# The last 64 rows of two weight matrices: from full rows on 64 partitions, loaded by GpSimd, to half rows on 128 partitions, loaded by SyncE

## The chip, the core and the metric

One core of a Trainium2 chip. The metric is the time of one execution in microseconds (us) of the device, taken as the median of several runs. Lower is better. Input and output tensors lie in HBM; the kernel brings them into the core's on-chip memory (SBUF, 128 partitions) with DMAs, which run on 16 DMA engines. A DMA is issued by an engine's queue: here SP (SyncE), ACT (ScalarE) and POOL (GpSimd). PE is TensorE, DVE is VectorE.

## The reference, cut to what matters

```python
# x: (8, 1, 448); 16 query heads on 8 KV heads of 256; cache of 4096, the last W = 1024 are used
q = (x @ wq).reshape(B, 1, Hq, Dh).transpose(0, 2, 1, 3)     # wq: 448 x 4096
k, v = the last W rows of the caches, each KV head for two query heads
p = softmax(q @ k^T * Dh**-0.5)
a = (p @ v) as (B, 1, 4096) @ wo                             # wo: 4096 x 448
h = gelu(layernorm(x) @ w1 + b1)                             # w1: 448 x 1792
b = h @ w2 + b2                                              # w2: 1792 x 448
g = sigmoid((x * gate_w).sum(-1))
out = g * a + (1 - g) * b
```

Everything is bfloat16. The row count of wq and w1, 448, is 3 x 128 + 64: the last 64 rows are what the change is about.

## The kernel before, in words

**Loads.** `plan` is a list of loads in a fixed order, each into one of `RING = 9` slots of 128 x 8192 elements (2 MB). `pump()` issues loads until nine are ahead of what has been consumed; `done()`, called where a slot has been read for the last time, frees one and pumps again. The order: the keys of group 0 (in two halves), w1, wq in two slots (two thirds of the main rows, then the last third), w2, then keys and values of 16 groups of four KV heads (values three groups behind the keys, `LAG`), and at the end wo in two slots and six pieces (L171 to L187). All these are issued by SP in the order of the plan. Each DMA from SP or ACT uses one of eight completion counters in turn, so an issue waits until the DMA eight places earlier has landed; it also waits for the last reader of the slot's previous content.

**Rows of wq and w1.** The first 384 rows (`DM`) stand three to a partition: partition p holds rows 3p, 3p+1, 3p+2 (L161, L162). The last 64 (`DT`) go through `ends` (L125): two DMAs of 32 rows each, onto partitions 64 to 95 and 96 to 127 (`ER = 64`), as full rows behind the main rows in the slot. They are issued by POOL. Ahead of each of them POOL issues a DMA of a few bytes into an unused tile, `side` (`step_over`, L117). Within 32 partitions the rows are permuted: partition 4i + j holds row 8j + i.

**Compute at the start.** `ends_of` (L248) puts the last 64 columns of x, in that permutation, into columns 64 to 127 of a zeroed row tile `xz`, and of the normed y into `yz`. `transposed` (L241) brings x (and y) to the partitions with four PE transposes: three for the main rows, one for the tail. `query` (L356) multiplies: 128 matmuls, of which the last 32 contract over partitions 64 to 127. `mlp_hidden` (L468) does the same for w1: 42 matmuls for the main rows and 14 for the tail (L482), then the bias and gelu on DVE and ACT.

**The loop.** For each group, `transpose_keys` turns 32 key tiles (64 PE transposes, copied out by ACT and DVE), `values(u - 3)` multiplies an earlier group's probabilities by its values, `scores` and `top` do the scores and their maxima. PE's program is written out by hand in this order. After the last group: `values`, `finish`, `spread_rows`, and `project` (L578), 128 matmuls against wo, each waiting for its piece. One DVE instruction (L599) applies the gate, and four DMAs store the result.

Of the kernel before, what the change touches and what calls it, by code (L numbers as in the profile page):

```python
# [11 lines left out]
BF16 = mybir.dt.bfloat16  # L12
# [5 lines left out]
def kernel(  # L18
# [15 lines left out]
    nc = tc.nc  # L34
    P = nc.NUM_PARTITIONS

    NB, Sq, D = A_x.shape
    _, Hkv, Sk, Dh = A_k_cache.shape
    HD = A_wq.shape[1]
# [4 lines left out]
    F = B_w1.shape[1]  # L44
    assert (NB, Sq, D, Hkv, Dh, Hq, W, F) == (8, 1, 448, 8, 256, 16, 1024, 1792)
    NJ = Dh // P
    NC = W // P
    NR = 3
    DM = NR * P
    DT = D - DM  # L50
    NF = F // P
    QUAD = 4
    RQ = QUAD * rep
    NQ = NB * Hkv // QUAD
# [8 lines left out]
    WO_PARTS = [[(0, NJ8)]] * (NHQ - 1) + [[(0, 4), (4, 6), (6, 8)]]  # L63
    RING = 9
    LAG = 3
    ER = P - DT
    BIG = 1e30
    qscale = float(Dh) ** -0.5

    xf = A_x.rearrange("b s d -> (b s) d")  # L70
# [3 lines left out]
    consts = ctx.enter_context(tc.tile_pool(name="consts", bufs=1))  # L74
# [36 lines left out]

        return load

    side = consts.tile([NB, 8, 32], BF16)
    turns = [0]

    def step_over():  # L117
        i = turns[0]
        turns[0] += 1
        nc.gpsimd.dma_start(  # L120
            side[:, 2 * i : 2 * i + 2, 0:16],
            xf[:, 0:32].rearrange("b (a n) -> b a n", a=2),
        )

    def ends(t, o, src):  # L125
        n = src.shape[1]
        for h in range(DT // 32):
            rows = src[DM + 32 * h : DM + 32 * h + 32, :]
            step_over()
            nc.gpsimd.dma_start(  # L130
                t[ER + 32 * h : ER + 32 * h + 32, o : o + n],
                rows.rearrange("(j i) n -> i j n", i=NB),
            )

    def rows_loader(pieces, tail=None):
        def load(t):
            o = 0
            for ap in pieces:
                n = 1
                for s in ap.shape[1:]:  # L140
                    n *= s
                dst = t[:, o : o + n]
                if len(ap.shape) == 3:
                    dst = dst.rearrange("p (a n) -> p a n", a=ap.shape[1])
                nc.sync.dma_start(dst, ap)  # L145
                o += n
            if tail is not None:
                ends(t, o, tail)

        return load  # L150

# [2 lines left out]
    def add(key, loader):  # L154
        index[key] = len(plan)
        plan.append(loader)
# [2 lines left out]
        add((name, u), kv_loader(src, u, parts))  # L159

    wq_m = A_wq[0:DM, :].rearrange("(p r) n -> p (r n)", r=NR)  # L161
    w1_m = B_w1[0:DM, :].rearrange("(p r) f -> p (r f)", r=NR)  # L162
    w2_v = B_w2.rearrange("(p c) n -> p (c n)", c=NF)
    wo_v = A_wo.rearrange("(q p j) n -> p q (j n)", p=P, j=NJ8)

    add_kv("k", A_k_cache, 0, parts=2)
    add(("w1",), rows_loader([w1_m], B_w1))
    add(("wq", 0), rows_loader([wq_m[:, 0 : 2 * HD]]))
    add(("wq", 1), rows_loader([wq_m[:, 2 * HD : 3 * HD]], A_wq))
    add(("w2",), rows_loader([w2_v]))  # L170
    for u in range(1, NQ):  # L171
        add_kv("k", A_k_cache, u)
# [17 lines left out]
        return slots[index[key]]  # L190

    x_sb = consts.tile([NB, D], BF16)
    ident = consts.tile([P, P], BF16)
    make_identity(nc, ident[:])
    pump()
    nc.scalar.dma_start(x_sb[:], xf)
    gw_b = consts.tile([NB, D], BF16)
    b2_r = consts.tile([1, D], BF16)
    b1_sb = consts.tile([P, NF], BF16)
    nc.scalar.dma_start(  # L200
        gw_b[:], gate_w.rearrange("(o d) -> o d", o=1).to_broadcast([NB, D])
    )
    nc.scalar.dma_start(b2_r[:], B_b2.rearrange("(o d) -> o d", o=1))
    nc.scalar.dma_start(b1_sb[:], B_b1.rearrange("(p c) -> p c", c=NF))

    ones_f = consts.tile([P, P], F32)
    nc.gpsimd.memset(ones_f[:], 1.0)

# [2 lines left out]
    PO = ps_po.tile([P, Dh], F32)  # L211
    nc.vector.memset(PO[:], 0.0)

    NX = NR + 1
    DQ = D // QUAD

    def quads(ps):
# [2 lines left out]
            for i in range(QUAD)  # L220
        ]

    xz = consts.tile([NB, P], BF16)
    yz = consts.tile([NB, P], BF16)
    nc.vector.memset(xz[:], 0.0)
    nc.vector.memset(yz[:], 0.0)
    xT = consts.tile([P, NX, NB], BF16)
    yT = consts.tile([P, NX, NB], BF16)
# [12 lines left out]
    def transposed(dst, src, srcz):  # L241
        tp = ps_misc.tile([P, NX, NB], BF16, tag="misc", name="tp")
        for r in range(NR):
            nc.tensor.transpose(tp[:, r, :], src[:, r:DM:NR], ident[:NB, :NB])
        nc.tensor.transpose(tp[:, NR, :], srcz[:], ident[:NB, :NB])
        nc.vector.tensor_copy(dst[:], tp[:])

    def ends_of(dst, src):  # L248
        nc.vector.tensor_copy(
            dst[:, ER:P].rearrange("b (h i j) -> b h i j", h=DT // 32, i=NB),  # L250
            src[:, DM:D].rearrange("b (h j i) -> b h i j", h=DT // 32, i=NB),
        )

    ends_of(xz, x_sb)
    transposed(xT, x_sb, xz)
    nc.vector.reduce_sum(
        sel[:], ident[:].rearrange("p (a s) -> p s a", a=QUAD)[:, 0:RQ, :], axis=AXIS.X
# [7 lines left out]
    rows = consts.tile([P, 1], F32)  # L265
# [11 lines left out]
    def norm_and_gate():  # L277
        stats = consts.tile([NB, nc.vector.BN_STATS_DIM], F32)
        nc.vector.bn_stats(stats[:], x_sb[:])
        mv = consts.tile([NB, nc.vector.BN_AGGR_DIM], F32)  # L280
        nc.vector.bn_aggr(mv[:], stats[:])
        eps_t = consts.tile([NB, 1], F32)
        nc.vector.memset(eps_t[:], 1e-5)
        rstd = consts.tile([NB, 1], F32)
        nc.scalar.activation(rstd[:], mv[:, 1:2], ACT.Sqrt, bias=eps_t[:], scale=1.0)
        nc.vector.reciprocal(rstd[:], rstd[:])
        y_sb = consts.tile([NB, D], BF16)
        nc.vector.tensor_scalar(
            y_sb[:],
            x_sb[:],  # L290
            scalar1=mv[:, 0:1],
            scalar2=rstd[:],
            op0=ALU.subtract,
            op1=ALU.mult,
        )
        ends_of(yz, y_sb)
        transposed(yT, y_sb, yz)
        prod = consts.tile([NB, D], F32)
        gl = consts.tile([NB, 1], F32)
        nc.vector.scalar_tensor_tensor(  # L300
            prod[:],
            in0=x_sb[:],
            scalar=1.0,
            in1=gw_b[:],
            op0=ALU.mult,
            op1=ALU.mult,
            accum_out=gl[:],
        )
        gth = consts.tile([NB, 1], F32)
        nc.scalar.activation(gth[:], gl[:], ACT.Tanh, scale=0.5)  # L310
        nc.vector.tensor_scalar(
            gg[:, 0:1], gth[:], 0.5, 0.5, op0=ALU.mult, op1=ALU.add
        )
        nc.vector.tensor_scalar(
            gg[:, 1:2], gth[:], -0.5, 0.5, op0=ALU.mult, op1=ALU.add
        )
        nc.vector.tensor_copy(
            spread[:, :, 0:NB],
            ident[0:NB, 0:NB]
            .rearrange("p (o b) -> p o b", o=1)  # L320
            .to_broadcast([NB, QUAD, NB]),
        )
        gp = ps_misc.tile([P, 2], F32, tag="misc", name="gp")
        nc.tensor.matmul(
            gp[:],
            lhsT=spread[:].rearrange("p i b -> p (i b)"),
            rhs=gg[:],
            start=True,
            stop=True,
        )  # L330
        nc.vector.tensor_copy(gg_s[:], gp[:])
# [24 lines left out]
    def query():  # L356
        qt = ps_misc.tile([P, Hq * NJ, NB], F32, tag="misc", name="qt")
        for r in range(NR + 1):
            w, o = slot("wq", r // 2), (r % 2) * HD
            p0 = ER if r == NR else 0  # L360
            for k in range(Hq * NJ):
                c = o + (k // NJ) * Dh + (k % NJ) * P
                nc.tensor.matmul(  # L363
                    qt[:, k, :],
                    lhsT=w[p0:P, c : c + P],
                    rhs=xT[p0:P, r, :],
                    start=(r == 0 and k == 0),
                    stop=(r == NR),
                    skip_group_check=True,
                )  # L370
        done(2)
        qv = qt[:].rearrange("p (g a i j) b -> p a j b g i", g=Hq // RQ, a=QUAD, i=rep)
        for a in range(QUAD):
            for j in range(NJ):
                nc.vector.tensor_scalar_mul(  # L375
                    qw[:, j, :, :, a, a * rep : (a + 1) * rep], qv[:, a, j], qscale
                )
# [90 lines left out]
    def mlp_hidden():  # L468
        hT = ps_misc.tile([P, NF, NB], F32, tag="misc", name="hT")
        w = slot("w1")  # L470
        for r in range(NR):
            o = r * F
            for c in range(NF):
                nc.tensor.matmul(
                    hT[:, c, :],
                    lhsT=w[:, o + c : o + F : NF],
                    rhs=yT[:, r, :],
                    start=(r == 0 and c == 0),
                    stop=False,
                    skip_group_check=True,  # L480
                )
        for c in range(NF):  # L482
            nc.tensor.matmul(
                hT[:, c, :],
                lhsT=w[ER:P, NR * F + c : NR * F + F : NF],
                rhs=yT[ER:P, NR, :],
                start=False,
                stop=True,
                skip_group_check=True,
            )  # L490
        done()
        z = consts.tile([P, NF, NB], F32)
        nc.vector.tensor_tensor(
# [146 lines left out]
```

## Time and profile before

| | |
|---|---|
| median of 3 runs | 197.0 us (196.94 to 197.16) |
| the profiled execution | 197.16 us, of which the span (first to last instruction) is 195.3 |
| PE busy | 148.5 us (76%), 2318 matmuls |
| DVE, ACT, POOL busy | 112.2 us (57%), 82.8 us (42%), 5.4 us (3%) |
| moved by DMA | 78.02 MB in 6840 packets, mean 400 GB/s |
| granted PE clock | 0.894 of full speed on the mean; 1.00 from 60 to 120 us, 0.50 from 176 us on |

How to read it: a row of digits cuts the span into 40 equal slices, and each digit is the busy share of one slice in tenths. The chain that ended last is followed back from the last instruction: at each step to what released it, or to the instruction before it on its engine. A DMA of 128 partitions is cut into packets, here one for each contiguous run in HBM; they are shared out over the 16 engines, eight packets to each, and each engine reports its own landing. The trace has the packets with their queue, size, start and duration, and the times of the landings; it doesn't name the DMA engine of a packet.

### The profile page before, as it was taken

What the parts mean: (1) busy time and instruction counts of PE and PEld (TensorE: products, weight loads), DVE (VectorE), ACT (ScalarE), POOL (GpSimd) and SP (SyncE); (2) the same over time, 40 slices, a digit from 0 to 9 for tenths busy, and PEclk for the clock granted to TensorE, in tenths of its full rate; (3) what the DMA queues carried; (4) which work ended last, traced back from release to release, by engine and by line L of the source; (5) the groups of instructions that cost most, each with busy time, mean ns of one, the idle gap of its engine ahead of it and who ended that gap; (6) DMA issues with size and microseconds to landing.
All of it is one profiled execution on the core that took longest, in us unless ns stands there. A gap on an engine that the chain in (4) does not pass through costs nothing.

```text
span 195.3 us, 5180 instructions
## 1 busy us (share of the span) xinstructions
PE 148.5 (76%) x2318; PEld 110.5 (57%) x2318; DVE 112.2 (57%) x257; ACT 82.8 (42%) x101; POOL 5.4 (3%) x15
## 2 busy tenths in 40 slices
PE   0398485999898988988777878787878696947652
PEld 0397454955767657675637464646465656535441
DVE  7532223677968678685846666666666666653100
ACT  2362000866848457382807272727272737320000
POOL 8200000000000000000000000000000000000000
PEclk9997555699999999999999999999999999985555
DMA  5999999999999999999999999999999999999830
GB/s 191 412 425 429 430 427 423 418 430 430 426 426 430 426 423 423 430 418 430 423 426 430 423 430 421 426 423 430 426 430 426 423 426 426 426 418 415 338 145 6
DMA packets 6840, 78.02 MB, mean 400 GB/s; under 512 B 1201, under 2 KB 1474, under 8 KB 2018
## 3 DMA queue, kind: packets, MB, share of 16 engines
q1 hardware_dynamic: 6224, 76.91, 93.3%
q0 software_dynamic: 384, 0.76, 1.0%
q8 instruction: 18, 0.29, 0.6%
q10 hardware_dynamic: 210, 0.02, 0.1%
q14 instruction: 4, 0.03, 0.0%
HBM read 77.68 MB, written 0.01 MB: 398 GB/s over the span
## 4 chain that ended last, share of the span: by engine, by line
DMA 86%; PE 8%; ACT 3%; issue 0%; SPq 0%; DVE 0%; ACTq 0%
DMA slot<-in_A_k_cache_dram 56%; DMA slot<-in_A_v_cache_dram 20%; DMA slot<-in_A_wo_dram 10%; PE ktp L346 5%; PE S_ps L384 2%; ACT kt L349 2%; ACT E L404 1%; PE PO L444 1%; PE sm L423 0%; PE A_ps L583 0%; DVE res L599 0%; PE sm L420 0%; SPq L145 0%; SPq L108 0%; ACTq L349 0%
## 5 line engine op out<-in xcount | busy, mean ns | idle before, releaser
L349 ACT COPY kt<-ktp 128x1024 bf16<-128x1024 bf16 x64 | 63.2, 1017 | 78.2 <-PE ktp L346 78.2
L346 PE MATMUL ktp<-ident,slot 128*128 128x128 bf16 x1024 | 72.0, 227 | 21.2 <-ACT kt L349 10.6
L346 PEld LDWEIGHTS <-slot 128*128 128x128 bf16 x1024 | 66.0, 104 | 28.1 <-issue 15.7
L351 DVE COPY kt<-ktp 128x1024 bf16<-128x1024 bf16 x64 | 41.3, 684 | 16.3 <-PE ktp L346 16.3
L384 PE MATMUL S_ps<-kt,qw 128*8 128x512 bf16 x256 | 32.3, 626 | 0.3 <-DVE qw L375 0.3
L396 DVE TENSOR_REDUCE nmx<-S_ps 128x1 f32<-128x1024 f32 x16 | 19.6, 1224 | 22.3 <-PE S_ps L384 22.3
L412 DVE STREAM_TRANSPOSE EB<-E 128x1024 bf16<-128x1024 bf16 x16 | 19.9, 1245 | 7.1 <-ACT E L404 6.9
L444 PE MATMUL PO<-slot,ET 128*8 128x256 bf16 x512 | 18.4, 290 | 3.0 <-DMA slot<-in_A_v_cache_dram 2.9
L404 ACT ACTIVATE E<-S_ps,nmx 128x1024 bf16<-128x1024 f32 x16 | 17.9, 1119 | 3.3 <-DVE nmx L397 3.3
L444 PEld LDWEIGHTS <-ET 128*8 128x8 bf16 x512 | 11.9, 90 | 6.2 <-issue 3.0
L384 PEld LDWEIGHTS <-qw 128*8 128x8 bf16 x256 | 7.2, 94 | 12.0 <-issue 10.4
L425 DVE CAST ET<-sm 128x256 bf16<-128x256 f32 x16 | 6.6, 415 | 0.7 <-PE sm L423 0.7
L363 PE MATMUL qt<-xT,slot 128*128 128x8 bf16 (+1 forms) x128 | 3.8, 167 | 3.4 <-DMA slot<-in_A_wq_dram 3.4
L583 PE MATMUL A_ps<-slot,oP 128*8 128x112 bf16 x128 | 4.1, 291 | 2.5 <-DMA slot<-in_A_wo_dram 2.3
L363 PEld LDWEIGHTS <-slot 128*128 128x128 bf16 (+1 forms) x128 | 3.6, 104 | 3.6 <-DMA slot<-in_A_wq_dram 3.6
L423 PE MATMUL sm<-selr,ones_f 128*128 128x8 f32 x32 | 5.3, 239 | 0.0
L464 DVE CAST oT<-sm 128x16 bf16<-128x16 f32 x16 | 3.5, 220 | 3.1 <-PE sm L461 3.1
L423 PEld LDWEIGHTS sm<-selr,ones_f 128*128 128x128 f32 x32 | 5.0, 196 | 0.4 <-issue 0.4
L583 PEld LDWEIGHTS <-oP 128*8 128x8 bf16 x128 | 2.9, 114 | 3.5 <-issue 3.5
L420 PE MATMUL sm<-EB,perm 128*128 128x256 bf16 x16 | 4.5, 279 | 0.3 <-DVE oT L464 0.3
L375 DVE TENSOR_SCALAR qw<-qt 128x32 bf16<-128x32 f32 x8 | 0.9, 180 | 5.2 <-PE qt L363 5.2
L599 DVE SCALAR_TENSOR_TENSOR res<-A_ps,gg_s,mixb 128x112 bf16<-128x112 f32 x1 | 0.3, 334 | 6.0 <-PE A_ps L583 6.0
(125 smaller groups left out, 77.0 us busy)
## 6 DMA issues: line engine op xcount, KB each, us to landing
slot<-in_A_v_cache_dram SPq DMA_DIRECT2D x16, 2048.0 KB, 38.7
slot<-in_A_k_cache_dram SPq DMA_DIRECT2D x15, 2048.0 KB, 37.0
slot<-in_A_wo_dram SPq DMA_DIRECT2D x3, 896.0 KB
slot<-in_A_k_cache_dram SPq DMA_DIRECT2D x2, 1024.0 KB, 7.8
slot<-in_A_wq_dram SPq DMA_DIRECT2D x1, 2048.0 KB
slot<-in_B_w_dram SPq DMA_DIRECT2D x1, 1568.0 KB
slot<-in_B_w_dram SPq DMA_DIRECT2D x1, 1344.0 KB, 12.1
slot<-in_A_wq_dram SPq DMA_DIRECT2D x1, 1024.0 KB
```

What stands on the lines that cost most here:

```text
L346: nc.tensor.transpose(ktp[:, c, :], kn[:, o : o + P], ident[:])
L349: nc.scalar.copy(dst, ktp[:])
L351: nc.vector.tensor_copy(dst, ktp[:])
L363: nc.tensor.matmul(qt[:, k, :], lhsT=w[p0:P, c : c + P], rhs=xT[p0:P, r, :], start=(r == 0 and k == 0), stop=(r == NR), skip_group_check=True,
L384: nc.tensor.matmul(S_ps[32 * a : 32 * a + RQ, hf * CH * SK : (hf + 1) * CH * SK], lhsT=qw[:, j, b, half, a, :], rhs=KT[hf][:, j, :, a::QUA ...
L396: nc.vector.reduce_max(nmx[:], S_ps[:], axis=AXIS.X, negate=True)
L404: nc.scalar.activation(E[:], S_ps[:], ACT.Exp, bias=nmx[:], scale=1.0, accum_out=rowsum[:])
L412: nc.vector.transpose(EB[:].rearrange("p c r -> p (c r)"), E[:])
L423: nc.tensor.matmul(sm[:, NCK, :], lhsT=ones_f[:], rhs=selr[:], start=True, stop=True)
L425: nc.vector.tensor_copy(ET[:], sm[:, 0:NCK, :])
L444: nc.tensor.matmul(PO[32 * t : 32 * t + RQ, :], lhsT=ET[:, c, 0:RQ], rhs=vn[:, c * Dh : (c + 1) * Dh], start=(c < QUAD), stop=(c >= NCK - ...
L583: nc.tensor.matmul(dst, lhsT=oP[:, j, q, :], rhs=w[:, o + cols.start : o + cols.stop], start=(q == 0 and j == 0), stop=(q == NHQ - 1 and j ...
```

## The change

The 64 tail rows of wq and w1 are no longer loaded by POOL. Each row is cut in half: a view with 128 half rows, half row 2r + h on partition 2r + h, is one more piece of the slot's load, issued by SP right behind the main rows. `side`, `step_over`, `ends` and `ends_of` go. Since partition 2r + h holds only half h of row r, x gets two transposed tail columns instead of one: in column h the value of row r stands on partition 2r + h, and the other partitions are zero. A matmul that needs half h takes column h and contracts over all 128 partitions. In `query` half the tail matmuls take either column; their number stays 32. In `mlp_hidden` a half row has 896 of the 1792 columns, so each half fills 64 of the 128 output partitions: 28 tail matmuls instead of 14. The identity is written a few lines later in the program.

```diff
-    def ends(t, o, src):
-        n = src.shape[1]
-        for h in range(DT // 32):
-            rows = src[DM + 32 * h : DM + 32 * h + 32, :]
-            step_over()
-            nc.gpsimd.dma_start(
-                t[ER + 32 * h : ER + 32 * h + 32, o : o + n],
-                rows.rearrange("(j i) n -> i j n", i=NB),
-            )
...
-            if tail is not None:
-                ends(t, o, tail)
...
+    wq_t = A_wq[DM:D, :].rearrange("r (h n) -> (r h) n", h=2)
+    w1_t = B_w1[DM:D, :].rearrange("r (h n) -> (r h) n", h=2)
...
-    add(("w1",), rows_loader([w1_m], B_w1))
+    add(("w1",), rows_loader([w1_m, w1_t]))
...
-    add(("wq", 1), rows_loader([wq_m[:, 2 * HD : 3 * HD]], A_wq))
+    add(("wq", 1), rows_loader([wq_m[:, 2 * HD : 3 * HD], wq_t]))
...
-    NX = NR + 1
+    NX = NR + 2
...
-        nc.tensor.transpose(tp[:, NR, :], srcz[:], ident[:NB, :NB])
+        for h in range(2):
+            nc.tensor.transpose(tp[:, NR + h, :], srcz[:, h, :], ident[:NB, :NB])
...
-    ends_of(xz, x_sb)
+    for h in range(2):
+        nc.vector.tensor_copy(xz[:, h, h::2], x_sb[:, DM:D])
...
-                    lhsT=w[p0:P, c : c + P],
-                    rhs=xT[p0:P, r, :],
+                    lhsT=w[:, o + c : o + c + P],
+                    rhs=xT[:, r + half, :],
...
-        for c in range(NF):
-            nc.tensor.matmul(
-                hT[:, c, :],
-                lhsT=w[ER:P, NR * F + c : NR * F + F : NF],
-                rhs=yT[ER:P, NR, :],
+        for h in range(2):
+            for c in range(NF):
+                nc.tensor.matmul(
+                    hT[64 * h : 64 * h + 64, c, :],
+                    lhsT=w[:, NR * F + c : NR * F + FH : NF],
+                    rhs=yT[:, NR + h, :],
```

The DMAs that this takes out and puts in:

| | before | after |
|---|---|---|
| POOL | four `side` DMAs of 0.5 KB, two of 112 KB (w1), two of 256 KB (wq) | none |
| SP | | 128 runs of 1,792 bytes behind w1; 128 runs of 4,096 bytes behind wq |

More of the change, by code (lines that the diff above doesn't have):

```diff
@@ L51 @@
     NF = F // P
+    FH = F // 2
+    HH = HD // 2
     QUAD = 4
@@ L65 @@
     LAG = 3
-    ER = P - DT
     BIG = 1e30
@@ L112, in kv_loader, with rows_loader @@
         return load
[L114 to L119, printed above, removed]
-        nc.gpsimd.dma_start(
-            side[:, 2 * i : 2 * i + 2, 0:16],
-            xf[:, 0:32].rearrange("b (a n) -> b a n", a=2),
-        )
-    def ends(t, o, src):
-        n = src.shape[1]
-        for h in range(DT // 32):
-            rows = src[DM + 32 * h : DM + 32 * h + 32, :]
-            step_over()
-            nc.gpsimd.dma_start(
-                t[ER + 32 * h : ER + 32 * h + 32, o : o + n],
-                rows.rearrange("(j i) n -> i j n", i=NB),
-            )
-    def rows_loader(pieces, tail=None):
+    def rows_loader(pieces):
         def load(t):
@@ L192 @@
     x_sb = consts.tile([NB, D], BF16)
-    ident = consts.tile([P, P], BF16)
-    make_identity(nc, ident[:])
     pump()
@@ L204 @@
     nc.scalar.dma_start(b1_sb[:], B_b1.rearrange("(p c) -> p c", c=NF))
+    ident = consts.tile([P, P], BF16)
+    make_identity(nc, ident[:])
     ones_f = consts.tile([P, P], F32)
@@ L221, in quads @@
         ]
-    xz = consts.tile([NB, P], BF16)
-    yz = consts.tile([NB, P], BF16)
+    xz = consts.tile([NB, 2, P], BF16)
+    yz = consts.tile([NB, 2, P], BF16)
     nc.vector.memset(xz[:], 0.0)
@@ L244, in transposed @@
             nc.tensor.transpose(tp[:, r, :], src[:, r:DM:NR], ident[:NB, :NB])
-        nc.tensor.transpose(tp[:, NR, :], srcz[:], ident[:NB, :NB])
+        for h in range(2):
+            nc.tensor.transpose(tp[:, NR + h, :], srcz[:, h, :], ident[:NB, :NB])
         nc.vector.tensor_copy(dst[:], tp[:])
[L248 to L252, printed above, removed]
-    ends_of(xz, x_sb)
+    for h in range(2):
+        nc.vector.tensor_copy(xz[:, h, h::2], x_sb[:, DM:D])
     transposed(xT, x_sb, xz)
@@ L295, in norm_and_gate @@
         )
-        ends_of(yz, y_sb)
+        for h in range(2):
+            nc.vector.tensor_copy(yz[:, h, h::2], y_sb[:, DM:D])
         transposed(yT, y_sb, yz)
@@ L359, in query @@
             w, o = slot("wq", r // 2), (r % 2) * HD
-            p0 = ER if r == NR else 0
             for k in range(Hq * NJ):
-                c = o + (k // NJ) * Dh + (k % NJ) * P
+                col = (k // NJ) * Dh + (k % NJ) * P
+                half, c = divmod(col, HH) if r == NR else (0, col)
                 nc.tensor.matmul(
                     qt[:, k, :],
-                    lhsT=w[p0:P, c : c + P],
-                    rhs=xT[p0:P, r, :],
+                    lhsT=w[:, o + c : o + c + P],
+                    rhs=xT[:, r + half, :],
                     start=(r == 0 and k == 0),
@@ L481, in mlp_hidden @@
                 )
-        for c in range(NF):
-            nc.tensor.matmul(
-                hT[:, c, :],
-                lhsT=w[ER:P, NR * F + c : NR * F + F : NF],
-                rhs=yT[ER:P, NR, :],
[L487 to L490, printed above, removed]
+        for h in range(2):
+            for c in range(NF):
[3 more added lines that the diff above has]
+                    rhs=yT[:, NR + h, :],
+                    start=False,
+                    stop=True,
+                    skip_group_check=True,
+                )
         done()
```

## The prediction

> **What bounds the kernel.** I read the slices of the span first, for where the DMA engines are full.
>
> ```profile
> DMA  5999999999999999999999999999999999999830
> GB/s 191 412 425 429 430 427 423 418 430 430 426 426 430 426 423 423 430 418 430 423 426 430 423 430 421 426 423 430 426 430 426 423 426 426 426 418 415 338 145 6
> ...
> q1 hardware_dynamic: 6224, 76.91, 93.3%
> q0 software_dynamic: 384, 0.76, 1.0%
> q8 instruction: 18, 0.29, 0.6%
> ```
>
> The reader sees 16 DMA engines full from the second slice to the 37th, then a ramp of two slices (8, 3) and not a cliff: the engines don't finish together. Queue q0 is POOL's, and its 0.76 MB are the 64 tail rows that the change moves. Next, the chain that ended last, its final pieces (start us, us, what).
>
> ```profile
> 132.45 39.10 DMA slot<-in_A_v_cache_dram
> 171.54 0.02 issue
> 171.56 19.88 DMA slot<-in_A_wo_dram
> 191.44 0.04 issue
> 191.49 0.39 PE A_ps L583 x8
> 191.87 0.02 issue
> 191.90 0.33 DVE res L599
> ```
>
> The last wo piece lands at 191.44; 0.39 us of TensorE, 0.33 us of VectorE and the store follow. So the time is set by when the slowest DMA engine finishes. Are the engines limited one by one, or by a total that they share? The windows answer (columns: us, PE, PEld, DVE, ACT, POOL busy, PE clock, DMA share, GB/s).
>
> ```profile
> 120.00:176.00 56.00, 43.04 (x650) 30.82 (x638) 35.39 (x72) 25.93 (x32) 0.00 (x0) 0.99 1.01 426
> ...
> 186.00:188.00 2.00, 1.17 (x43) 0.75 (x33) 0.00 (x0) 0.00 (x0) 0.00 (x0) 0.50 0.40 164
> 188.00:190.00 2.00, 0.77 (x32) 0.74 (x32) 0.00 (x0) 0.00 (x0) 0.00 (x0) 0.50 0.29 113
> ```
>
> At 186 to 188 us 0.40 of the engines are busy and move 164 GB/s: 164 / 0.40 = 410 for a full set, against 426 / 1.01 = 422 with all at work. A lone engine is no faster. The packet records agree: wo packets of 7,168 bytes have a median of 275 ns from 173 to 181 us and 273 ns from 187 to 189 us. Each engine has its own rate, and bytes given to one engine can't be made up by another.
>
> Which engines end last? Every DMA of 128 partitions reports 16 landings, one for each engine. From the trace's landing records, first landing in us, then all 16 as offsets from it:
>
> ```
> half of K group 0    8.3   0.0 to 0.9
> w1, 384 rows        11.5   0.0 0.1 0.1 0.2 0.2 0.2 0.3 0.4 | 2.1 2.1 2.2 2.2 2.2 2.4 2.5 2.7
> w2                  22.7   0.0 0.1 0.2 0.2 0.2 0.2 0.4 0.6 | 3.6 3.6 3.7 3.7 3.7 3.9 3.9 5.2
> a K or V group     100.9   0.0 0.1 0.2 0.3 1.1 1.7 1.8 2.0 | 3.6 3.9 5.2 5.3 5.3 5.3 5.5 6.8
> last wo piece      183.2   0.0 0.1 0.1 0.3 1.0 2.6 3.3 3.4 | 3.5 3.8 6.6 6.7 6.7 6.7 6.9 8.3
> ```
>
> Eight engines fall 3.6 us behind between 9 and 22 us and never recover. That is when POOL's packets run (starts from 6.7 to 19.8 us), and the DMA rows show who issued them:
>
> ```profile
> slot<-in_A_wq_dram POOLq DMA_DIRECT2D x2, 256.0 KB, 13.2
> slot<-in_B_w_dram POOLq DMA_DIRECT2D x2, 112.0 KB, 7.0
> side<-in_A_x_dram POOLq DMA_DIRECT2D x4, 0.5 KB, 7.1
> ```
>
> The packet records hold 64 packets of 8,192 bytes at 309 ns and 32 of 7,168 at 272 ns for these rows: 19.8 + 8.7 = 28.5 us of engine time. On 8 engines that is **3.56 us each**, which is the split seen (3.6). On all 16 it would be 1.78 us and no split. So the four tail DMAs all sit on one half of the engines; the little side DMAs between them take the turns of the other half.
>
> The other lateness is not of the change: 18 instruction packets of 16 KB (q8), median 1.07 us. An engine that serves one is 1.3 to 1.5 us later from then on (offset 3.9 becomes 5.3). One engine of the late half gets a third one at 183.9 us: that is the step from 6.9 to 8.3.
>
> **The change, part by part.**
>
> *DMAs.* Removed: 3.56 us on each engine of the late half; on the early half the side DMAs (32 packets of 64 bytes, 11 ns: under 0.1 us each). Added, on all 16 engines, by SP: w1_t, 128 runs of 1,792 bytes, and wq_t, 128 of 4,096. A 1,792-byte packet takes 74 ns in the wo rows. One of 4,096 isn't in the trace: between 140 ns (3,584 bytes) and 272 (7,168), on the line through the first two 159 ns, and I take that. Eight of each per engine: 8 x 74 + 8 x 159 = **1.86 us** (1.71 to 2.77 by the bounds). Late half: 1.86 - 3.56 = -1.70. Early half: +1.8.
>
> So the last landing is the later of two: the late half at 183.2 + 8.3 - 1.7 = 189.8, the early half at 183.2 + 3.4 + 1.86 = 188.5. **189.8 against 191.5: 1.7 us gained**; by the bounds 1.85 down to 0.8.
>
> *SP's queue.* Two more issues (0.33 to 0.6 us each) stand ahead of w2 and K 1. Each issue reuses a completion counter and waits for the DMA eight earlier, so everything behind shifts by two counters: the second wq part waits for the first half of K 0 (landed 6.0), K 1 for the small b1 load (9.9; issued from 6.39 before). Queued behind K 1 are K 2, K 3, V 0 and all later loads. Backlog at 9.9 us: 9.0 MB issued (K 0, w1, wq, w2) less 8 us x 0.42 = 3.4 moved leaves 5.6 MB, 13 us of work. Cost nothing; without that cover it would be 9.9 - 6.4 = 3.5 us.
>
> *POOL.* Loses eight issues (4.6 us); the last one stood before ones_f, whose first reader is the softmax sum at 38 us. Nothing. The identity is written after the loads in the program, but POOL has nothing else to do: nothing.
>
> *TensorE.* One more transpose for each of x and y, and 28 hT matmuls of 64 columns for 14 with 64 rows. The 14 took 1.00 us from 17.93; the new form isn't shown: from nothing to another 2.6 us (the 42 full ones), I take 1.0. Query keeps its 128 matmuls, the last 32 over 128 partitions instead of 64. All this ends before query, which waited 2.94 us for wq until 21.87; wq lands earlier now. Even if TensorE ran 1 to 2 us late here, the loads don't wait for it: they have 25 us of backlog at 22 us.
>
> *VectorE.* One more copy of 8x64 for x and for y (0.19, 0.21 us; with step two unseen, bounded by 0.5, the 8x448 row), wider clears of xz and yz: hidden in the same way.
>
> *The tail end.* The last V group lands at 181.4 now. Late half -1.7 gives 179.7, early half 177.8 + 1.86 = 179.7. TensorE then needs 3.87 us to its first projection matmul (181.40 to 185.27) and about 4 x 0.93 + 0.4 for all 128: done by 187.7, 2 us before the last wo landing. DMA stays last.
>
> [...] This trace runs at 426 and shows the rate following the number of busy engines.
>
> **The sum.** The profiled execution took 197.16 us (span 195.3, 1.9 around it), 0.16 above the median of the runs. 197.16 - 1.70 = 195.46 for a run like it, **195.3** against the median of 197.0.
>
> **Rivals.**
> 1. *An instruction packet falls elsewhere.* TensorE's program gets 16 more matmuls with their weight loads, so the packets are asked for a little earlier. If the third one misses the last engine, the late half ends at 183.2 + 6.9 - 1.7 = 188.4, and the early half at 188.5 is last: 3.0 us gained, 194.0. If it hits another engine at 6.9, or the last of the early half, 189.9 to 190.0: within my forecast. For: the packet at 183.9 comes late. Against: the engines take turns in a fixed order through the trace.
> 2. *Half the gain.* The 4,096-byte packets cost as much as 7,168-byte ones, or one engine gets one more instruction packet near the end (189.8 + 1.4 = 191.2, 0.3 gained): 196.0 to 196.7.
> 3. *It doesn't do what it says*: a shared limit binds, total bytes are the same, 197.0. Against: the windows above.
> 4. *Slower.* The POOL bytes sit on the half that ends early, and the late half is late for another reason that stays. Then the late half gains 1.86 us of packets and loses none: 191.5 + 1.86, 198.9. It decides from the point where the late half carries less than 1.86 us of POOL's packets. For: the records name no engine. Against: size and moment of the split both fit POOL's packets.
>
> **How the numbers follow.** Forecast 195.3 (195.0 to 195.7): 0.62. Rival 1, 194.0: 0.12. Rival 2: 0.12 (a good 196.0 to 196.5 mostly). Rival 3: 0.08. Rival 4: 0.06. The range takes in the first three, 193.8 to 196.6. A measurement of this kernel tells about 0.2% (0.4 us) from no change: faster 0.86, same 0.08, slower 0.06.
>
> **What would show it.** Right: the offsets of w2's landings fall from 5.2 to under 2 us with no gap of 3.6 in the middle; POOL's queue gone; the first engine ends wo near 185.0 instead of 183.2 and the last near 189.8; the ramp at the end steeper. Wrong: the gap is still there, or the early half ends where it did, or SP's stream lets the DMA row fall under 9 before the 37th slice.

## The result, and the profile after

The changed kernel takes **195.51 us** (median of 4 runs, 195.46 to 195.75) against 197.08 before (4 runs, 196.94 to 197.20): a ratio of 0.9923, 95% interval 0.9906 to 0.9940. The forecast was 195.3. The profiled execution took 195.75 us, with a span of 193.9.

The page of the changed kernel, DMA slices and queues:

```profile
DMA  5999999999999999999999999999999999999950
GB/s 194 418 426 416 445 424 424 426 426 416 419 426 429 423 423 426 423 431 429 429 426 419 429 426 417 423 426 426 426 429 423 423 416 433 429 429 406 409 202 7
...
q1 hardware_dynamic: 6512, 77.67, 95.1%
q8 instruction: 18, 0.29, 0.6%
```

The engines are full for one slice longer (37 in a row instead of 36, then 5, where it was 8 and 3), and POOL's queue q0 is gone; its bytes are in q1, and the total of 78.02 MB is the same. The chain that ended last, its end:

```profile
130.83 39.15 DMA slot<-in_A_v_cache_dram
169.98 0.02 issue
170.00 20.23 DMA slot<-in_A_wo_dram
190.23 0.04 issue
190.27 0.38 PE A_ps L561 x7
190.66 0.02 issue
190.68 0.33 DVE res L577
```

It is the same chain, and its last load lands at 190.23 instead of 191.44. The windows at the end (columns as before; the last two are the DMA share and GB/s) show the same work pressed together. Scaled to a full set the first two move 380 to 395 GB/s (303 / 0.77, 206 / 0.54):

```profile
184.00:186.00 2.00, 0.93 (x43) 0.69 (x35) 0.29 (x1) 0.00 (x0) 0.00 (x0) 0.50 0.77 303
186.00:188.00 2.00, 0.73 (x36) 0.55 (x28) 0.00 (x0) 0.00 (x0) 0.00 (x0) 0.50 0.54 206
188.00:190.00 2.00, 1.73 (x56) 1.23 (x56) 0.00 (x0) 0.00 (x0) 0.00 (x0) 0.50 0.10 32
```

From 186 to 188 us 0.54 of the engines still work, where it was 0.40; from 188 to 190 only 0.10, where it was 0.29. The landing records, as in the prediction (first landing, then the 16 offsets):

```
w1, 384 rows        11.3   0.0 0.0 0.0 0.1 0.1 0.1 0.1 0.1 0.1 0.1 0.2 0.2 0.3 0.3 0.3 0.4
w2                  24.4   0.0 0.0 0.0 0.0 0.1 0.1 0.1 0.1 0.1 0.1 0.1 0.2 0.2 0.2 0.4 1.9
a K or V group      97.9   0.0 0.0 0.0 0.1 0.2 0.4 0.7 1.0 1.6 1.6 1.7 1.7 1.7 1.8 1.8 3.4
last wo piece      185.3   0.0 0.0 0.0 0.1 0.2 0.4 0.7 2.0 3.1 3.2 3.2 3.2 3.2 3.3 3.5 5.0
```

The gap of 3.6 us in the middle is gone. What is left goes with the instruction packets: steps of 1.4 to 1.6 us after those of 16 KB, one engine after the other and one engine with a third, and steps of 0.6 to 1.0 us after three of 8 KB (at 32.5, 84.6 and 118.1 us, in a queue of their own).

### The profile page after: what moved, and what is told of

The parts are those of the page before. It is cut to its first block, busy times and chain, and to the rows that moved or that the text cites. A ratio compares the mean times of both kernels' runs of the same rounds, so it can differ in the third digit from the quotient of the medians.

```text
span 193.9 us, 5200 instructions
## 1 busy us (share of the span) xinstructions
PE 147.3 (76%) x2334; PEld 109.1 (56%) x2334; DVE 112.4 (58%) x259; ACT 82.7 (43%) x101; POOL 0.9 (0%) x7
## 2 busy tenths in 40 slices
DMA packets 6744, 78.02 MB, mean 402 GB/s; under 512 B 945, under 2 KB 1346, under 8 KB 1986
## 4 chain that ended last, share of the span: by engine, by line
DMA 86%; PE 6%; ACT 5%; ACTq 1%; issue 0%; DVE 0%; SPq 0%
DMA slot<-in_A_k_cache_dram 52%; DMA slot<-in_A_v_cache_dram 20%; DMA slot<-in_A_wo_dram 10%; DMA b_sb<-in_B_b_dram 4%; ACT kt L326 3%; PE ktp L323 3%; PE S_ps L361 2%; ACT E L381 2%; PE PO L421 1%; ACTq L174 0%; PE sm L400 0%; PE A_ps L561 0%; DVE res L577 0%; PE sm L397 0%; ACTq L178 0%
## 5 line engine op out<-in xcount | busy, mean ns | idle before, releaser
L323 PE MATMUL ktp<-ident,slot 128*128 128x128 bf16 x1024 | 69.0, 221 | 23.7 <-DMA slot<-in_A_k_cache_dram 11.7
L340 PE MATMUL qt<-xT,slot 128*128 128x8 bf16 x128 | 3.6, 168 | 0.4 <-DVE z L471 0.4
```

Source lines behind the costliest of these rows:

```text
L323: nc.tensor.transpose(ktp[:, c, :], kn[:, o : o + P], ident[:])
L340: nc.tensor.matmul(qt[:, k, :], lhsT=w[:, o + c : o + c + P], rhs=xT[:, r + half, :], start=(r == 0 and k == 0), stop=(r == NR), skip_grou ...
```

## The experiments

Three explanations were on the table. *Engine theory*, that of the prediction: each engine has its own rate, and the half that carried all tail packets set the end. *Queue theory*: POOL's queue costs by itself. *Start-up theory*: the gain is TensorE's shorter wait for wq. A fourth, the *home theory*, had to be formed on the way. "First half" and "late half" are the two sets of eight engines that the landings of before show.

### 1. POOL's tail DMAs spread over both halves

```diff
         for h in range(DT // 32):
             rows = src[DM + 32 * h : DM + 32 * h + 32, :]
-            step_over()
             nc.gpsimd.dma_start(
```

> The kernel before without its four side DMAs; POOL still issues the four tail DMAs as full rows on 64 partitions. Engine theory (bytes of each DMA engine decide): without the side DMAs the tail DMAs take the two halves of the engines in turn, 1.78 us of packets on each engine instead of 3.56 on one half, so the gap in the middle of w2's landings goes and the time is that of the changed kernel, 195.5 us (195.2 to 195.8). Queue theory (POOL's queue costs, wherever its packets run): four of eight POOL DMAs stay with all their bytes, 196.8 to 197.1. Start-up theory (the gain comes from TensorE's shorter wait for wq or from the layout): TensorE's work is that of before, 197.0.

**197.11 us** (11 runs, 196.89 to 197.62; ratio to before 1.0008, interval 1.0000 to 1.0017). A miss for the engine theory, and what both the queue theory and the start-up theory said; experiment 4 answers these two. Yet what the engine theory says of the halves came true: the landings have no gap (w2: 0.0 to 1.6 us; the last wo piece 0.0 to 4.7). All engines are late instead: the first one ends at 186.7, where the changed kernel has 185.3. The window in which the tail runs tells why. First before, then this run:

```profile
6.00:16.00 10.00, 7.77 (x82) 7.49 (x82) 4.46 (x13) 4.55 (x6) 0.30 (x2) 1.00 1.02 420
```

```profile
6.00:16.00 10.00, 7.06 (x71) 6.37 (x71) 4.34 (x13) 5.01 (x6) 0.00 (x0) 1.00 1.05 356
```

The engines are as busy (1.02, 1.05) and move 356 GB/s instead of 420. The packets themselves are slower: tail packets of 8,192 bytes have a median of 397 ns, not 309, and SP's packets beside them stretch too. Added up over the run, POOL's tail packets took 8.2 us more than in before and SP's 20.6, the latter in loads that start in the first 27 us. Those 28.8 us are 1.8 us for each of 16 engines. That eats the gain of the even spread.

### 2. The other half

```diff
-            step_over()
             nc.gpsimd.dma_start(
                 t[ER + 32 * h : ER + 32 * h + 32, o : o + n],
                 rows.rearrange("(j i) n -> i j n", i=NB),
             )
+            step_over()
```

> The kernel before with each side DMA behind its tail DMA instead of ahead of it, so that all four tail DMAs take the half of the engines that the side DMAs had. Engine theory: the half that was late loses 3.56 us (191.5 to 187.9 at the last landing), the other gains 3.56 (186.6 to 190.2): 1.3 us faster than before, 195.8 us (195.5 to 196.2), and the eight engines that fall behind early are now those with fewer instruction packets, so the spread of the last landings is under 7.5 us instead of 8.3. Queue theory: the same POOL DMAs in another order, 197.0. If the halves were alike: 197.0 too.

**200.09 us** (6 runs, 199.01 to 200.90; ratio 1.0152, 1.0124 to 1.0180), the opposite sign of what the engine theory said. The tail packets are now slower still (8,192 bytes: median 418 ns), and for longer:

```profile
6.00:16.00 10.00, 7.60 (x70) 7.16 (x70) 4.56 (x13) 4.55 (x6) 0.31 (x2) 1.00 1.04 317
16.00:22.00 6.00, 3.64 (x56) 3.54 (x56) 0.60 (x3) 0.59 (x1) 0.00 (x0) 0.68 1.03 314
```

Full engines, 317 and 314 GB/s. So the halves aren't alike for these bytes. The *home theory* was formed here, as a supposition: each half goes with 64 of the partitions, the late half with 64 to 127; a packet that a half writes into the other half's partitions runs slow, and so does the stream of loads beside it. No trace names the engine of a packet; what runs can show is the packets' time for each pairing of half and partitions. Before, with the tail on partitions 64 to 127 and on the late half, is the pairing with 309 ns.

### 3. and 4. The same two, with the tail on partitions 0 to 63

```diff
-    ER = P - DT
+    ER = 0
...
-            p0 = ER if r == NR else 0
+            p0, p1 = (ER, ER + DT) if r == NR else (0, P)
```

with the slices `ER:P` made `ER : ER + DT`. Run 3 has the side DMAs as in before (late half), run 4 as in experiment 2 (first half).

> The kernel before with its tail rows on partitions 0 to 63 instead of 64 to 127, side DMAs where they were, so the same half of the engines. Home theory (the eight engines whose share of every 128-partition load is partitions 64 to 127 are the late half; a packet written by one half of the engines into the other half's partitions runs slow, and slows the stream beside it): the tail packets, now in the other half's partitions, take about 400 ns instead of 309 and the rate falls to 300 GB/s or so while they run; 199 to 201 us. Engine theory alone: the same bytes on the same engines, 197.0. POOL-order theory (a tail DMA that starts first in POOL's queue is slow, wherever it writes): the order is that of before, 197.0.

> As the run before, and the side DMAs behind the tail DMAs, so the tail goes through the other half of the engines, and into partitions 0 to 63. Home theory: those are that half's own partitions, so the packets are back at 272 and 309 ns, and the engine theory's sum for the other half holds: last landing 190.2 instead of 191.5, 195.8 us (195.4 to 196.2). POOL-order theory: slow packets as in the run with the same order, 200. Engine theory alone: 195.8 too; only the run beside it tells the two apart.

Run 3: **200.73 us** (6 runs, 200.31 to 201.40; ratio 1.0208, 1.0178 to 1.0238). Run 4: **195.91 us** (12 runs, 195.58 to 197.57; ratio 0.9965, 0.9942 to 0.9988). The windows, run 3 and then run 4:

```profile
6.00:16.00 10.00, 7.59 (x70) 7.17 (x70) 4.56 (x13) 4.55 (x6) 0.30 (x2) 1.00 1.07 331
```

```profile
6.00:16.00 10.00, 7.75 (x88) 7.41 (x88) 4.46 (x13) 5.02 (x6) 0.30 (x2) 1.00 1.03 423
```

And POOL's queue on the pages: the same bytes, and the time they took as a share of 16 engines. In the order of experiments 2 (first half, partitions 64 to 127), 3 (late half, 0 to 63) and 4 (first half, 0 to 63); before (late half, 64 to 127) had 1.0%:

```profile
q0 software_dynamic: 384, 0.76, 1.3%
```

```profile
q0 software_dynamic: 384, 0.76, 1.3%
```

```profile
q0 software_dynamic: 384, 0.76, 1.0%
```

| median ns of an 8,192-byte tail packet, time | partitions 64 to 127 | partitions 0 to 63 |
|---|---|---|
| late half | 309, 197.0 us (before) | 409, 200.7 us |
| first half | 418, 200.1 us | 309, 195.9 us |

Neither the half nor the partitions nor POOL's order decides, only the pairing of half and partitions: 309 ns in two cells, 409 and 418 in the other two. That is what the home theory forecast for runs 3 and 4; which engine writes which partitions, and why a packet is slow, no run shows. "At home" below means the two pairings with 309 ns. In them the engine theory's sum holds too. For run 4 that sum takes 3.56 us off the late half and puts them on the first, so that the last landing comes 1.3 us earlier, at 190.2, and the time is 195.8. The profile has it at 171.94 + 18.52 = 190.46:

```profile
171.94 18.52 DMA slot<-in_A_wo_dram
```

The same eight POOL DMAs as in before are in run 4, so the queue theory doesn't explain its gain. Nor does the start-up theory: TensorE starts the query at 20.9 us in run 4 and in experiment 1 alike, 1.0 us ahead of before, and the times are 195.91 and 197.11.

### 5. The changed kernel's half rows, issued by POOL

```diff
-                nc.sync.dma_start(dst, ap)
+                eng = nc.gpsimd if ap is w1_t or ap is wq_t else nc.sync
+                eng.dma_start(dst, ap)
```

(and the identity made ahead of the loads, so that POOL's issues, some 0.56 us each in before, don't hold it up)

> The changed kernel with its two half-row DMAs issued by POOL instead of SP. Engine theory: the packets spread over all 16 engines as before, 195.5 us (195.3 to 195.8). Queue theory: the cost of POOL's queue comes back, 196.5 to 197.1.

**196.13 us** (5 runs, 196.06 to 196.19; ratio 0.9956, 0.9944 to 0.9967), between the two. The packets are not slow (4,096 bytes: 159 ns), and the last load lands where it does in the changed kernel:

```profile
170.66 19.48 DMA slot<-in_A_wo_dram
```

170.66 + 19.48 = 190.14, against 190.23. The 0.6 us is lost behind it: from the last packet of the store to the end of the span it takes 2.14 us here, 1.52 in the changed kernel and 1.69 in before. So queue theory is wrong for the stream of loads. There is a small cost at the program's end, but that it is POOL's is not shown: experiments 8 to 10, from which POOL's DMAs are gone too, have 1.61 to 1.83.

### 6. w1's tail as before, wq's by SP

Against the changed kernel, with `side`, `step_over`, `ends` and `ends_of` of before:

```diff
-    add(("w1",), rows_loader([w1_m, w1_t]))
+    add(("w1",), rows_loader([w1_m], B_w1))
...
-        for h in range(2):
-            nc.vector.tensor_copy(yz[:, h, h::2], y_sb[:, DM:D])
+        ends_of(yz, y_sb)
...
-                    lhsT=w[:, NR * F + c : NR * F + FH : NF],
-                    rhs=yT[:, NR + h, :],
+                lhsT=w[ER:P, NR * F + c : NR * F + F : NF],
+                rhs=yT[ER:P, NR, :],
```

> The changed kernel with the w1 tail alone as before (POOL, full rows on 64 partitions, a side DMA ahead of each), wq's by SP as half rows. Engine theory: the late half carries 4 packets of 272 ns more and 8 of 74 fewer on each engine, +0.5 us against the changed kernel, 196.0 us (195.8 to 196.3). Queue theory: any POOL traffic brings half or more of the cost by the number of DMAs, 196.3 to 197.0. Shared limit: 195.5, the total is the same.

**195.80 us** (5 runs, 195.77 to 195.95; ratio 0.9942, 0.9929 to 0.9955): 0.3 above the changed kernel, where 0.5 was expected; the two were not run side by side, and the intervals of their ratios overlap. The w2 landings show a split of 0.6 us (0.2 to 0.8 and 0.9), near the 0.5 of the sum. At the last landing the profile shows no difference (190.24). So the early split is as the engine theory has it, and a cost at the end is not shown.

### 7. w1's tail at home on the first half

As experiment 6, but through the half with fewer instruction packets (in the last wo landings of before, two engines of the first half stand at 3.3 and 3.4 us, six of the late half at 6.6 to 8.3), and onto partitions 0 to 63, the pairing of run 4:

```diff
-    ER = P - DT
+    ER = 0
...
-            step_over()
             nc.gpsimd.dma_start(
                 t[ER + 32 * h : ER + 32 * h + 32, o : o + n],
                 rows.rearrange("(j i) n -> i j n", i=NB),
             )
+            step_over()
```

> The changed kernel with w1's tail alone by POOL, full rows on partitions 0 to 63, through the half of the engines that gets fewer instruction packets; wq's by SP as half rows. Engine and home theory together: the late half loses 0.59 us of w1 packets (last landing 190.3 to 189.7), the other gains 0.5 (188.7 to 189.2): 0.5 faster than the changed kernel, 194.9 us (194.7 to 195.3), the best so far. Without the home theory (its packets slow): 195.5 or more. Shared limit: 195.5.

**194.97 us** (7 runs, 194.77 to 195.98; ratio 0.9918, 0.9889 to 0.9947). Beside the changed kernel on one chip:

> The best version so far beside the changed kernel on one chip: 0.5 us faster than it, 194.9 to 195.0 us.

> The changed kernel itself, for the comparison on one chip: 195.5 us.

**194.90 us** (194.78 to 195.04; ratio to before 0.9896, 0.9883 to 0.9910) against **195.63** (195.52 to 195.71; 0.9932, 0.9920 to 0.9945). The ranges don't meet: 0.7 us faster than the change itself. The chains of the two profiles, first this kernel and then the changed one:

```profile
170.35 19.08 DMA slot<-in_A_wo_dram
```

```profile
170.25 19.95 DMA slot<-in_A_wo_dram
```

The last load lands at 189.43 and at 190.20. This is the sum of the prediction carried on: bytes taken off the engines that end last.

### 8. Fewer TensorE instructions

```diff
-        for r in range(NR + 1):          # query
+        for r in range(NR, NR + 1):
...
-        for r in range(NR):              # mlp_hidden
+        for r in range(1):
...
-        for c in range(NF):              # mlp_out
+        for c in (0, NF - 1):
```

> The changed kernel with 344 PE instructions left out at the start: the query is made from the 64 tail rows alone, w1's first third and tail alone, and 2 of 14 slices of w2. All loads stay. Instruction-packet theory (the last engine ends 1.5 us after the next one because it alone serves a third instruction packet before the end): the 17th packet is asked for 344 instructions later, behind the last load; the last landing's offset falls from 5.0 to 3.4, 194.0 us (193.8 to 194.4). If the last engine is late for a reason of its own: offset still 5.0, 195.5.

In the profiled execution the landings are what the theory says: the last wo piece's offsets end at 3.4 instead of 5.0, the last load lands at 188.72, and the page has one instruction packet less, the last one at 189.3 us, behind the last load. Its time, 194.46 us, is half a microsecond above the 194.0 expected; of that 0.3 us is a longer end behind the last load (3.96 us, 3.66 in the changed kernel).

```profile
q8 instruction: 17, 0.28, 0.6%
```

But the median of the 6 runs is **194.97 us** (194.46 to 195.04; ratio 0.9909, 0.9882 to 0.9936), another half a microsecond above. So the third packet is what makes one engine last in the profiled execution of the changed kernel; that removing it is worth 1.5 us in every execution is not shown. Before has such a spread too: two of its 18 runs here took 195.54 and 195.66, the others 196.86 to 197.19, and no profile shows why.

### 9. and 10. The tail at home without POOL

As experiment 7, with w1's tail issued by SP: in two DMAs of 32 rows,

```diff
-            nc.gpsimd.dma_start(
+            nc.sync.dma_start(
                 t[ER + 32 * h : ER + 32 * h + 32, o : o + n],
                 rows.rearrange("(j i) n -> i j n", i=NB),
             )
-            step_over()
```

then as one of 64 rows (partition 8i + j holds row 8j + i):

```diff
+        nc.sync.dma_start(
+            t[ER : ER + DT, o : o + n],
+            src[DM:D, :].rearrange("(j i) n -> i j n", i=NB),
+        )
```

> As the run with w1's tail alone on partitions 0 to 63, but those two DMAs come from SP; no POOL DMA and no side DMA is left. If SP's DMAs of 8 source rows go to the eight engines whose home is partitions 0 to 63: the same landings as in that run, packets at 272 ns, 194.8 to 195.0 us. If they go to the other eight: slow packets, and the late half gets them, 196 to 197.

> As the run with w1's tail by SP through eight engines, as one DMA of 64 rows instead of two of 32, so that the completion counters of all later DMAs are those of the changed kernel. Engine and home theory: last wo landing near 189.1 in its profile as in that run, against 190.2 in the changed kernel. If the 0.4 us that run lost between its last load and its end came from the counters: 194.5 to 194.8 us, the best. If it came with SP's eight-engine DMAs: 195.3 to 195.6 again.

**195.49 us** (5 runs, 195.33 to 195.66) and **195.68 us** (195.36 to 195.83). The packets are not slow in the first (3,584 bytes: all 64 take 140 ns), and its last load lands at 189.17, 0.3 us ahead of experiment 7, with a time 0.6 us longer. The loss is behind the last load: 4.39 us from there to the end of the span, 3.66 in the changed kernel. Issuing SP's two store DMAs takes 0.35 us of it (1.07 us instead of 0.72).

In the second the packets are slow. The same 64 of 3,584 bytes have a median of 169 ns and reach 318, and the rate falls in the third and fourth slice. GB/s on the two pages, the first kernel and then the second:

```profile
GB/s 184 424 432 415 439 436 415 416 430 423 430 423 427 427 430 420 433 418 427 427 427 427 420 427 425 433 423 427 420 423 430 420 433 423 430 430 407 412 207 3
```

```profile
GB/s 193 418 375 396 430 423 425 423 430 430 430 423 433 420 427 423 427 418 430 420 427 427 430 430 411 433 427 427 430 427 423 427 430 420 430 427 408 416 264 16
```

Yet the bytes go onto partitions 0 to 63 in both, and the last landings have the same pattern (first seven offsets 0.0 0.3 1.2 1.4 1.4 1.4 2.3 in the first, 0.0 0.3 1.3 1.4 1.5 1.5 2.3 in the second), as if the same eight engines carried them. What differs is the place within the half: the rows 8j + i of one i lie on partitions 4i to 4i + 3 and 32 + 4i to 32 + 4i + 3 in the first, on 8i to 8i + 7 in the second. So the half of the partitions alone doesn't set a packet's time: 140 ns with the one placing, 169 with the other. Why is not shown; the traces name no engine.

The second's last load lands at 189.92, 0.75 us behind the first's, and from there to the end it takes 3.66 us, as in the changed kernel. So in its profile the loss of the first is gone with the counters put back, and the slow packets take the gain instead. As the edit changed the counters, the number of DMAs and the partitions at once, it doesn't show that the counters were the cause. One DMA by SP with the first's placing of the rows was not tried.

## Why the prediction was right

**The mechanism.** The chain ends in the same loads, the split of 3.6 us is gone, the first engine ends later (185.3) and the last earlier (190.23). Experiments 4 and 7 move bytes from the late engines to the others and get the sums' results (195.9 and 194.9 us); the start-up theory falls with experiments 1 and 4, which start the query at the same time and differ by 1.2 us.

**The sizes.** 1.70 us were forecast for the last landing; the profiles show 191.44 - 190.23 = 1.21. The late half lost its 3.56, and the new packets cost what was said (161 ns for 4,096 bytes, 74 for 1,792: 1.88 us). The rest of the stream is not quite as it was: the first engine moved from 183.2 to 185.3, by 2.1 and not by 1.86, of which 1.7 was there by w2's landing (22.7 to 24.4) and the remainder grew slowly over the 150 us behind it; and the last engine's lateness by instruction packets is 5.0, not the 4.8 that 8.3 - 3.5 gave. Those two make most of the 0.5. In return the end of the program is shorter by 0.17 us (1.69 to 1.52 from the last store packet on), which wasn't in the sum; 1.21 + 0.17 is the 1.4 between the profiled executions, and the medians differ by 1.57.

**The step that failed, and the luck.** "On all 16 it would be 1.78 us and no split" took the engines as alike, so that it only mattered how many bytes each one got. Experiment 1 did just that and gained nothing; experiment 2 put the bytes on the half that the sum preferred and lost 3 us. The bytes' destination counts as well: 309 or 409 ns for the same packets on the late half. The change was priced rightly because the packets of its half rows, loaded onto all 128 partitions, were not slowed: 161 and 74 ns, where the sum has 159 and 74. That was luck: the prediction never asked where the packets are written, and the same sum was off by 1.6 us for experiment 1 and by 4.3 us for experiment 2. The side DMAs of before do more than take turns: with them the tail's 8,192-byte packets took 309 ns, without them 397. Rival 4, the slower one, asked on which engines POOL's bytes sit, but it too priced them by count alone.

**Smaller steps.** The 28 hT matmuls took 2.99 us, not 2.0, for 1.00 before (107 ns each instead of 71); they stayed hidden, as query started at 20.43 instead of 21.87. K 1's issue fell back to 9.06 us (9.9 said) from 6.39, and the DMA slices stay full: its cover was there. Rival 1 did not happen: the third instruction packet came 3 us earlier (180.7 instead of 183.9) and again made one of the late engines the last. Rival 3 did not happen either: with the same 78.02 MB, and 426 GB/s before and 425 after from 120 to 176 us, evening out the engines gave its 1.57 us. The transfers to half of the partitions didn't spread over 16 engines in before: w2's landings have the gap, 0.6 to 3.6 us.

## What to carry to other kernels

When DMA is the bound, read the 16 landings of a DMA and not only its last: the gap that split them in two here (3.6 us) came from bytes that only some engines carried, and the late set's surplus, less what every engine then got (3.56 less 1.86), was about the gain of evening out (1.57). Before moving such bytes, look at where they are written: the same tail packets took 309 ns in two pairings of half and partitions and 409 and 418 in the other two, while the half rows on 128 partitions took what the sum had for them (161 ns, against 159). Then give the odd bytes to the engines that end first, which was worth another 0.7 us in experiment 7.

## What the runs showed of the hardware

- Tail packets beside a full stream, in the two pairings of half and partitions that weren't at home (experiments 2 and 3): medians of 409 to 418 ns instead of 309 for 8,192 bytes and of 346 to 347.5 instead of 272 for 7,168, and the whole core's rate at 317 and 331 GB/s instead of 420 with full engines (6 to 16 us). Within one half, 3,584 bytes took a median of 169 ns instead of 140 when they lay on other partitions of it (experiment 10).
- Instruction packets of 16 KB: 18 in the trace, the first 17 some 10 us apart (17.7 to 180.7 us in the changed kernel), 17 in all when 344 TensorE instructions were left out. The landings step by 1.3 to 1.6 us after them, on eight of the 16 engines. Their lengths come again after eight packets (changed kernel: 1100, 1087, 1311, 1018, 1074, 1078, 1060, 1099 ns, then 1099, 1094, 1018, 1018, 1073, 1078, 1061, 1099), as if eight engines took turns in a fixed order. By that estimate 16 packets give each of the eight two, and the 17th makes one engine last: its offset is 5.0 us where the next has 3.5, and 3.4 is the last one in experiment 8.
- From the last store packet to the end of the span: 1.52 to 1.83 us without POOL DMAs, 1.62 to 1.69 with four or eight small ones, 2.14 with two of 128 partitions (one run).
